# One attention-plus-SwiGLU kernel: a reordered opening and a later place for batch 1's key mixing

## The chip, the cores and the metric

The kernel runs on one core of a Trainium2 chip. The metric is the device time of one execution in microseconds (us). One execution was recorded by the profiler; its span, from the first to the last instruction, is shorter than its device time, because something lies around the span.

## The reference

There are four batches of 8 heads, 768 positions of 64 numbers each, and an 8 x 8 matrix `sort_net` per head. Five rounds of exp and of row and column normalisation turn `sort_net` into P. P mixes the eight blocks of 96 positions of K and of V; each block of Q then attends to the mixed block, and a SwiGLU feed-forward layer takes all heads side by side.

```
for _ in range(5):
    P = exp(P - max(P)); P = P / sum(P, axis=-1); P = P / sum(P, axis=-2)
k_sorted = einsum('bhij,bhjcd->bhicd', P, k_blocks)
v_sorted = einsum('bhij,bhjcd->bhicd', P, v_blocks)
attn = softmax(scale * q_block @ k_sorted_block.T)
x = (attn @ v_sorted_block)           # 3072 tokens x 512 (8 heads x 64)
out = (silu(x @ w_gate) * (x @ w_val)) @ w_out     # 512 -> 1536 -> 512
```

## The kernel before

**Stages.** The tokens fall into eight passes of 384, `ffn(0)` to `ffn(7)`: pass n is half n % 2 of batch n // 2. A pass needs `xts[(b, half)]`, the attention output with features on partitions. Attention runs in units, `(b, u)` for u from 0 to 7: four blocks of two heads. A unit goes through `qk` (scores, 8 matmuls, then an exp on ScalarE), `av` (8 matmuls, then a reciprocal and a multiplication on VectorE), and a transpose (4 matmuls and a copy) into `xts`. Units 0 to 3 of a batch feed its first pass, units 4 to 7 its second.

**Mixing.** Before a batch's units, K and Q are mixed and transposed together by `kq_chunk` (L230: two matmuls for each of n positions into one PSUM tile, then one copy `drain` on VectorE, "v", or ScalarE, "s"), and V by `v_chunk` (L240: one matmul for each of n features, then a drain in the same way). Batch 0 is mixed in the opening, lines 456 to 474. Batch 1 is mixed inside the second pass: `kqs(1, ...)` gives three pairs of key chunks, and `vs(v_chunk, 16, ...)` four chunks of values.

**What sets the order.** TensorE and GpSimd follow the program exactly (a manual schedule). In the opening VectorE and ScalarE do too; from line 525 on they are ordered by the framework's scheduler, which is not spelled out in the code. In the passes, `merge(main, side)` (L551) puts side work between the steps of a pass: each main step has a cost (0.65 for a gate or value group of four matmuls, 0.87 for a third of an output tile), the costs are added up, and a side step is put in as soon as the sum reaches its due time. These costs only set the order. In `ffn(1)` the outputs of pass 0 (`outp`, L384) come after the value group m = 3, 7 and 11, in three parts each.

**PSUM.** Tags "a" and "b" are two double-bank tiles, shared by the mixing chunks, scores and AV results; each new use waits until the last one is drained. "gen" is three banks, used in turn by gate, value and some output tiles. "x" is one bank, for transposes.

**Transfers.** GpSimd issues all loads, with a cast to bf16, in program order: V, Q and K of batch 0, the gate and value weights in 12 pieces, K, V and Q of batch 1 (`load_q(1, 0, C)`, L144), the output weights `wo_sb` in one piece (L145), and then K of batches 2 and 3 (`kp`, L95). The four copies `vch<-v` of batch 1 (L120) follow on GpSimd.

**Unread matmuls.** `fill(idle_ps, n)` (L415) issues n matmuls of 128 x 512 whose results nobody reads.

```
kq_chunk(1, ...) reads kq_tiles[1]: rows 0-63 from load_k(1), rows 64-127 from load_q(1)
outp(n, t3, part) reads h_tiles[n] and wo_sb
```

Of the kernel before, what the change touches and what calls it, by code (L numbers as in the profile page):

```python
# [17 lines left out]
def kernel(  # L18
# [158 lines left out]
    def pair_tile(name, tag):  # L177
        return psum.tile([128, 1024], FP32, name=name, tag=tag)

    def bank_tile(name, tag="gen"):  # L180
        return psum.tile([128, 512], FP32, name=name, tag=tag, bufs=3 if tag == "gen" else 1)
# [29 lines left out]
    def drain(eng, dst, src):  # L211
        if eng == "v":
            nc.vector.tensor_copy(dst, src)  # L213
        else:
            nc.scalar.copy(dst, src)  # L215
# [3 lines left out]
    def kqt_tile(b):  # L219
        if b not in kqts:  # L220
            kqts[b] = kqp.tile([128, 2 * H2 * NB * C + 32], BF16, name=f"kqt{b}", tag="kqt")
        return kqts[b]
# [3 lines left out]
    def chunk_tile(name, n, tag):  # L226
        return pair_tile(name, tag) if n == 2 else bank_tile(name, tag)

    def kq_chunk(b, at, n, eng, tag):
        dst = kqt_tile(b)[:, 0:2 * GI * C].rearrange("p (n c) -> p n c", c=C)  # L230
        rm = rmix[b].rearrange("p two a g i -> p two (a g i)")
        tp = chunk_tile("tkq", n // 8, tag).rearrange("p (l n) -> p l n", n=2 * GI)
        for lc in range(n):
            for two in range(2):
                nc.tensor.matmul(tp[two * D:(two + 1) * D, lc, :],  # L235
                                 lhsT=kq_tiles[b][:, at + lc, :],
                                 rhs=rm[:, two, :], start=True, stop=True)
        drain(eng, dst[:, :, at:at + n], tp.transpose([0, 2, 1]))
# [25 lines left out]
    def scores(b, u, tag):  # L264
        half, g = divmod(u, H2)
        k_sb, k_at, q_sb, q_at = ((kqts[b], 0, kqts[b], GI * C) if b < 2 else
                                  (kqts["p"], (b - 2) * GI * C, kqts["q"], (b - 2) * GI * C))
        if tag == "gen":
            wide = None
            pss = [bank_tile("qk"), bank_tile("qk")]  # L270
        else:
            wide = pair_tile("qk", tag).rearrange("p (two n) -> p two n", two=2)
            pss = [wide[:, 0], wide[:, 1]]
        for i4 in range(4):
            at = (g * NB + half * 4 + i4) * C
            for two in range(2):
                lo = two * D
                nc.tensor.matmul(pss[two][:, i4 * C:(i4 + 1) * C],  # L278
                                 lhsT=k_sb[lo:lo + D, k_at + at:k_at + at + 128],
                                 rhs=q_sb[lo:lo + D, q_at + at:q_at + at + C],  # L280
                                 start=True, stop=True)
        return wide, pss

    def exps(b, u, wide, pss):
        n = ecount[0] % 8
        ecount[0] += 2
        if wide is None:
            for two in range(2):
                nc.scalar.activation(e_all[:, n + two, 0:4 * C], pss[two][0:C, 0:4 * C], AF.Exp, scale=scale)
        else:  # L290
            nc.scalar.activation(e_all[:, n:n + 2, 0:4 * C], wide[0:C, :, 0:4 * C], AF.Exp, scale=scale)  # L291
        es[(b, u)] = [e_all[:, n, :], e_all[:, n + 1, :]]

    def qk(b, u, tag="b"):
        exps(b, u, *scores(b, u, tag))

    def av(b, u, tag="a"):
        half, g = divmod(u, H2)
        vt = vts[b // 2][:, b % 2].rearrange("p (h i) e -> p h i e", h=H)
        av_ps = pair_tile("av_ps", tag).rearrange("p (two n) -> p two n", two=2)  # L300
        o = av_ps[:, :, 0:4 * (D + 1)].rearrange("p two (i e) -> p two i e", e=D + 1)
        for two in range(2):
            e = es[(b, u)][two]
            for i4 in range(4):
                nc.tensor.matmul(o[:, two, i4, :], lhsT=e[:, i4 * C:i4 * C + 128],  # L305
                                 rhs=vt[:, 2 * g + two, half * 4 + i4, :],
                                 start=True, stop=True)
        r_sb = ssp.tile([C, 2, 4, 1], FP32, name="r_sb", tag="r")
        nc.vector.reciprocal(r_sb, o[0:C, :, :, D:D + 1])  # L309
        st = ssp.tile([C, 4, 2, D], BF16, name="st", tag="st")  # L310
        nc.vector.tensor_tensor(st.rearrange("p i two d -> p two i d"), o[0:C, :, :, 0:D],  # L311
                                r_sb.to_broadcast([C, 2, 4, D]), op=ALU.mult)
        sts[(b, u)] = st

    def xt_tile(tag, n):
        bank = psum.tile([128, 1024], BF16, name="x_ps", tag=tag, bufs=3 if tag == "gen" else 1)
        return bank[:, 0:n * 4 * C].rearrange("p (g a b) -> p g a b", g=n, b=C)

    def x_to(dst, b, u):
        st = sts.pop((b, u))  # L320
        for i4 in range(4):
            nc.tensor.transpose(dst[:, i4, :], st[:, i4].rearrange("p a b -> p (a b)"),
                                ident[0:C, 0:C])
# [89 lines left out]
    idle_ps = bank_tile("idle_ps", "x")  # L413

    def fill(tile, n):  # L415
        for _ in range(n):
            nc.tensor.matmul(tile, lhsT=warm_sb[:, 0:128], rhs=warm_sb, start=True, stop=True)  # L417
# [37 lines left out]
    fill(idle_ps, 2)  # L455
    v_chunk(0, 0, 8, "v", "gen")
    v_chunk(0, 8, 16, "s", "a")
    fill(idle_ps, 2)
    v_chunk(0, 24, 16, "v", "b")
    fill(idle_ps, 2)  # L460
    v_chunk(0, 40, 8, "s", "gen")
    v_chunk(0, 48, 8, "v", "gen")
    v_chunk(0, 56, 8, "s", "gen")
    kq_chunk(0, 0, 16, "v", "a")
    kq_chunk(0, 16, 16, "s", "b")
    fill(idle_ps, 1)
    kq_chunk(0, 32, 8, "s", "gen")
    kq_chunk(0, 40, 8, "s", "gen")
    kq_chunk(0, 48, 8, "v", "gen")
    fill(idle_ps, 1)  # L470
    kq_chunk(0, 56, 16, "v", "b")
    fill(idle_ps, 1)
    kq_chunk(0, 72, 16, "s", "a")
    kq_chunk(0, 88, 8, "v", "gen")
    for b in range(1, B):
        mix_of(b, w_sb)
# [4 lines left out]
    idle_ps = bank_tile("idle_ps")  # L481
# [3 lines left out]
    av(0, 1, "b")  # L485
    fill(idle_ps, 1)
    xts[(0, 0)] = xtp.tile([128, H2, TW], BF16, name="xt0_0", tag="xt")
    x01 = xt_tile("x", 2)
    x_to(x01[:, 0], 0, 0)
    fill(idle_ps, 1)  # L490
    qk(0, 3, "gen")
    av(0, 2, "a")
    x_to(x01[:, 1], 0, 1)
    drain("s", xts[(0, 0)][:, 0:2, :], x01.rearrange("p g a b -> p g (a b)"))
    fill(idle_ps, 2)
# [32 lines left out]
    def units(b, us, ats):  # L528
        us = list(us)
        todo = []  # L530
        for n, at in enumerate(ats):
            u, u2 = us[2 * n:2 * n + 2]
            held = []
            todo.append((at, lambda u=u, u2=u2, held=held: (qk(b, u, "b"), held.append(scores(b, u2, "a")))))
            todo.append((at + 1.3, lambda u2=u2, held=held: exps(b, u2, *held[0])))
            for w, tag, t in ((u, "b", 1.9), (u2, "a", 3.6)):
                if b < 2:
                    todo.append((at + t, lambda w=w, tag=tag: av(b, w, tag)))
                    todo.append((at + t + 3.1, lambda w=w: drain("v", *xtr(b, w))))
                else:  # L540
                    todo.append((at + t, lambda w=w, tag=tag: (av(b, w, tag), x_dma(b, w))))
        return todo

    def kqs(b, ats):
        return [(at, lambda n=n: (kq_chunk(b, n * 32, 16, "v", "b"), kq_chunk(b, n * 32 + 16, 16, "s", "a")))
                for n, at in enumerate(ats)]

    def vs(f, size, ats):
        return [(at, lambda m=m: f(1, m * size, size, "sv"[m % 2], "ba"[m % 2])) for m, at in enumerate(ats)]

    def merge(main, side):  # L551
        done, k = 0.0, 0
        side = sorted(side, key=lambda t: t[0])
        for c, f in main:
            f()
            done += c
            while k < len(side) and side[k][0] <= done:
                side[k][1]()
                k += 1
        while k < len(side):  # L560
            side[k][1]()
            k += 1

    def ffn(n):
        todo = []
        for m in range(NFC):
            if n > 0 or m > 1:
                todo.append((0.65, lambda m=m: gate(n, m)))
            if n > 0 or m > 0:
                todo.append((0.65, lambda m=m: value(n, m)))  # L570
            if n > 0 and m % 4 == 3:
                for part in range(3):
                    todo.append((0.87, lambda m=m, part=part: outp(n - 1, m // 4, part)))
        return todo
# [7 lines left out]
    q_cast(3)  # L582
    both = slice(0, 128)
    merge(ffn(0), units(0, range(4, 8), (0.0, 5.6)))
    merge(ffn(1), kqs(1, (0.3, 2.6, 4.9)) + vs(v_chunk, 16, (6.2, 7.3, 8.4, 9.5)) + units(1, range(4), (11.0, 15.6)))
    for s in range(4):
        copy_v(nc.gpsimd, 1, both, s)
    nc.vector.memset(kqt_tile("p")[:, 2 * GI * C:], 0.0)
# [42 lines left out]
```

The softmax here doesn't subtract the row's maximum and nothing guards it: scores larger than these inputs give would overflow.

## Time and profile before

| what | value |
|---|---|
| five executions | 254.05, 254.5, 254.67, 255.87, 256.28 us |
| their median | 254.67 us |
| the profiled execution | 254.5 us |
| its span | 252.4 us |
| TensorE busy | 240.7 us (95% of the span) |
| VectorE busy | 159.4 us (63%) |
| ScalarE busy | 110.5 us (44%) |
| GpSimd busy | 52.0 us (21%) |
| granted TensorE clock | 1.000 |

Stretches of the trace, in us from the span's start:

| stretch | what TensorE does | TensorE busy, us |
|---|---|---|
| 12.71 to 21.37 | batch 0's mixing with unread matmuls | 8.54 |
| 21.37 to 28.50 | first four units, first gate and value groups | 6.44 |
| 28.50 to 47.14 | pass 0 with units 4 to 7, then gate 0 of pass 1 | 18.50 |
| 47.14 to 49.19 | waits | 0.00 |
| 49.19 to 57.55 | batch 1's key mixing between the groups of pass 1 | 8.32 |
| 57.55 to 66.90 | outputs of pass 0, value mixing, first scores of batch 1 | 9.09 |
| 66.90 to 81.14 | the rest of pass 1 | 14.18 |
| 81.14 to 252.4 | passes 2 to 7 and the last outputs | 167.78 |

A line of the timeline gives start, duration, engine, source line, operation, output and inputs, the number of instructions and, in brackets, how long the engine was idle before it and what ended that. A matmul's end is modelled, so the duration of a group runs a little past the start of the next one; the time that a group takes is read from start to start.

### The profile page before, as it was taken

The page shows a single profiled execution, that of the slowest core. Times are in us where ns is not written, and L with a number is a line of the kernel's source. Part 1 is how long each engine was busy: PE and PEld are TensorE (multiplying, and loading weights), DVE is VectorE, ACT ScalarE, POOL GpSimd, SP SyncE. Part 2 cuts the span into 40 slices and gives each one's busy share as a digit, 9 for nine tenths or more (in the row PEclk, how much of TensorE's full clock was granted, in tenths as well). Part 3 has the DMA queues.
Part 4 walks back from the last instruction along what each step waited for, and adds up shares of the span by engine and source line. Part 5 has one row for each costly group of instructions (what it writes and reads, how often), then busy time and mean ns, then how long its engine had stood idle before and what let it go on. Part 6 is the DMA issues. An engine that isn't in the chain of part 4 may idle for free.

```text
span 252.4 us, 6061 instructions
## 1 busy us (share of the span) xinstructions
PE 240.7 (95%) x2574; PEld 143.3 (57%) x2574; DVE 159.4 (63%) x342; ACT 110.5 (44%) x187; POOL 52.0 (21%) x46
## 2 busy tenths in 40 slices
PE   5799999699999999999999999999999999999994
PEld 5275566466555666656656555555555565555543
DVE  6767788685757866758668458545854685456700
ACT  3966644255542543455544433443434243332311
POOL 7838430799069100000000000000000000000000
PEclk9999999999999999999999999999999999999999
DMA  5949999999999176110113112111111111100122
GB/s 101 212 78 161 196 216 219 194 222 216 230 156 153 42 168 130 42 44 3 42 21 85 42 41 57 51 44 32 60 57 42 34 57 57 44 7 34 44 83 84
DMA packets 37866, 23.98 MB, mean 95 GB/s; under 512 B 26064, under 2 KB 34000, under 8 KB 37328
## 3 DMA queue, kind: packets, MB, share of 16 engines
q0 software_dynamic: 21328, 14.16, 38.3%
q1 hardware_dynamic: 16512, 9.45, 13.0%
q8 instruction: 20, 0.33, 0.5%
q14 instruction: 6, 0.05, 0.1%
HBM read 28.32 MB, written 7.86 MB: 143 GB/s over the span
## 4 chain that ended last, share of the span: by engine, by line
PE 74%; DMA 15%; DVE 3%; POOL 3%; issue 2%; ACT 1%; DVEq 0%; POOLq 0%
PE o_ps L391 23%; PE v_ps L374 21%; PE g_ps L356 20%; DMA kq<-in_q_dram 7%; DMA kq<-in_k_dram 5%; DMA wg_sb<-in_moe_w_gate_dram 4%; PE tkq L235 3%; PE av_ps L305 2%; PE qk L278 2%; PE tv L257 1%; DVE gs_sb L366 1%; PE o_ps L407 1%; DVE vt L213 1%; POOL wg_sb L107 1%; POOL wv_sb L107 1%
## 5 line engine op out<-in xcount | busy, mean ns | idle before, releaser
L366 DVE SCALAR_TENSOR_TENSOR gs_sb<-th_sb,g_ps 128x384 bf16<-128x384 bf16 x96 | 52.8, 550 | 52.9 <-ACT th_sb L364 50.7
L374 PE MATMUL v_ps<-xt,wv_sb 128*128 128x384 bf16 x380 | 77.3, 326 | 0.3
L356 PE MATMUL g_ps<-xt,wg_sb 128*128 128x384 bf16 x376 | 76.5, 326 | 0.0
L364 ACT ACTIVATE th_sb<-g_ps 128x384 bf16<-128x384 f32 x96 | 47.2, 491 | 57.9 <-PE g_ps L356 54.9
L391 PE MATMUL o_ps<-wo_sb,h 128*128 128x512 bf16 x276 | 64.5, 379 | 0.0
L379 DVE SCALAR_TENSOR_TENSOR h<-v_ps,gs_sb 128x384 bf16<-128x384 f32 x96 | 53.3, 555 | 6.9 <-DVE gs_sb L366 0.5
L374 PEld LDWEIGHTS <-wv_sb 128*128 128x128 bf16 x380 | 35.4, 97 | 23.6 <-issue 1.5
L356 PEld LDWEIGHTS <-wg_sb 128*128 128x128 bf16 x376 | 34.6, 97 | 22.9
L391 PEld LDWEIGHTS <-h 128*128 128x128 bf16 x276 | 26.0, 98 | 27.7
L396 ACT COPY o_sb<-o_ps 128x512 f32<-128x512 f32 x23 | 13.5, 586 | 51.4 <-PE o_ps L391 51.4
L120 POOL COPY vch<-v 64x1536 bf16<-64x1536 bf16 (+1 forms) x10 | 28.1, 2850 | 18.4 <-DMA v<-in_v_dram 10.1
L291 ACT ACTIVATE e_all<-qk 96x768 bf16<-96x768 f32 x30 | 22.5, 802 | 6.2 <-PE qk L278 6.2
L311 DVE TENSOR_TENSOR st<-av_ps,r_sb 96x512 bf16<-96x512 f32 x32 | 21.7, 679 | 0.2
L305 PEld LDWEIGHTS <-e_all 96*128 96x128 bf16 x256 | 12.2, 98 | 5.1 <-ACT e_all L291 0.9
L305 PE MATMUL av_ps<-vt,e_all 96*128 96x65 bf16 x256 | 13.5, 194 | 0.2 <-ACT e_all L291 0.2
L213 DVE CAST vt<-tv 96x1024 bf16<-96x1024 f32 (+1 forms) x9 | 9.8, 1101 | 4.3 <-PE tv L247 4.3
L215 ACT CAST vt<-tv 96x1024 bf16<-96x1024 f32 (+1 forms) x9 | 9.1, 1030 | 5.6 <-PE tv L247 2.9
L309 DVE RECIPROCAL r_sb<-av_ps 96x8 f32<-96x8 f32 x32 | 6.4, 199 | 6.2 <-PE av_ps L305 6.1
L235 PE MATMUL tkq<-rmix,kq 128*64 128x64 bf16 x384 | 7.4, 197 | 2.0 <-DMA kq<-in_q_dram 2.0
L417 PE MATMUL idle_ps<-warm_sb 128*128 128x512 bf16 x30 | 9.2, 394 | 0.0
L215 ACT CAST kqt<-tkq 128x1024 bf16<-128x1024 f32 (+1 forms) x7 | 6.0, 894 | 7.0 <-PE tkq L235 7.0
L213 DVE CAST kqt<-tkq 128x1024 bf16<-128x1024 f32 (+1 forms) x7 | 7.5, 1069 | 2.6 <-PE tkq L235 2.4
(79 smaller groups left out, 135.6 us busy)
## 6 DMA issues: line engine op xcount, KB each, us to landing
out_dram<-o_sb SPq DMA_DIRECT2D x23, 256.0 KB, 2.0
v<-in_v_dram POOLq DMA_DIRECT2D x3, 768.0 KB, 14.3
kq<-in_q_dram POOLq DMA_DIRECT2D x2, 768.0 KB, 13.6
wg_sb<-in_moe_w_gate_dram POOLq DMA_DIRECT2D x6, 256.0 KB, 9.4
wv_sb<-in_moe_w_val_dram POOLq DMA_DIRECT2D x6, 256.0 KB, 10.0
wo_sb<-in_moe_w_out_dram POOLq DMA_DIRECT2D x1, 1536.0 KB, 23.6
kp<-in_k_dram POOLq DMA_DIRECT2D x2, 768.0 KB, 26.9
q_scr<-in_q_dram POOLq DMA_DIRECT2D x2, 768.0 KB, 21.1
```

What stands on the lines that cost most here:

```text
L120: eng.tensor_copy(dst, src.transpose([0, 2, 1]))
L213: nc.vector.tensor_copy(dst, src)
L215: nc.scalar.copy(dst, src)
L291: nc.scalar.activation(e_all[:, n:n + 2, 0:4 * C], wide[0:C, :, 0:4 * C], AF.Exp, scale=scale)
L305: nc.tensor.matmul(o[:, two, i4, :], lhsT=e[:, i4 * C:i4 * C + 128], rhs=vt[:, 2 * g + two, half * 4 + i4, :], start=True, stop=True)
L311: nc.vector.tensor_tensor(st.rearrange("p i two d -> p two i d"), o[0:C, :, :, 0:D], r_sb.to_broadcast([C, 2, 4, D]), op=ALU.mult)
L356: nc.tensor.matmul(g_ps, lhsT=wg_sb[:, kc, ts(m, 128)], rhs=xt[:, kc, :], start=(kc == 0), stop=(kc == NKC - 1))
L364: nc.scalar.activation(th_sb, g_ps, AF.Tanh, scale=0.5)
L366: nc.vector.scalar_tensor_tensor(gs_sb, th_sb, 1.0, g_ps, op0=ALU.add, op1=ALU.mult)
L374: nc.tensor.matmul(v_ps, lhsT=wv_sb[:, kc, ts(m, 128)], rhs=xt[:, kc, :], start=(kc == 0), stop=(kc == NKC - 1))
L379: nc.vector.scalar_tensor_tensor(h_tiles[n][:, m, :], v_ps, 0.5, gs_tiles.pop(m), op0=ALU.mult, op1=ALU.mult)
L391: nc.tensor.matmul(o_ps, lhsT=h_w[:, m, ts(t3, 128)], rhs=wo_sb[:, m, :], start=(m == 0), stop=(m == NFC - 1))
```

## The change

There are three edits, all of them to the order in which TensorE is given work; no matmul that is read is added or removed.

1. In the opening the two fills of two between the value chunks go (four matmuls), and one more unread matmul is put ahead of `kq_chunk(0, 32, ...)`, of `kq_chunk(0, 56, ...)` and of `kq_chunk(0, 88, ...)` (three matmuls).
2. The scores of unit 3 and the AV of unit 2 now come ahead of the transposes of unit 0; one unread matmul between them goes.
3. In `ffn(1)` the due times of batch 1's key mixing go from 0.3, 2.6, 4.9 to 2.4, 4.6, 6.8, those of its value mixing from 6.2, 7.3, 8.4, 9.5 to 7.8, 8.8, 9.8, 10.8, and those of its two unit pairs from 11.0 and 15.6 to 11.7 and 16.2.

```diff
     v_chunk(0, 0, 8, "v", "gen")
     v_chunk(0, 8, 16, "s", "a")
-    fill(idle_ps, 2)
     v_chunk(0, 24, 16, "v", "b")
-    fill(idle_ps, 2)
     v_chunk(0, 40, 8, "s", "gen")
     v_chunk(0, 48, 8, "v", "gen")
     v_chunk(0, 56, 8, "s", "gen")
     kq_chunk(0, 0, 16, "v", "a")
     kq_chunk(0, 16, 16, "s", "b")
-    fill(idle_ps, 1)
+    fill(idle_ps, 2)
     kq_chunk(0, 32, 8, "s", "gen")
     kq_chunk(0, 40, 8, "s", "gen")
     kq_chunk(0, 48, 8, "v", "gen")
-    fill(idle_ps, 1)
+    fill(idle_ps, 2)
     kq_chunk(0, 56, 16, "v", "b")
     fill(idle_ps, 1)
     kq_chunk(0, 72, 16, "s", "a")
+    fill(idle_ps, 1)
     kq_chunk(0, 88, 8, "v", "gen")
...
     xts[(0, 0)] = xtp.tile([128, H2, TW], BF16, name="xt0_0", tag="xt")
+    qk(0, 3, "gen")
+    av(0, 2, "a")
     x01 = xt_tile("x", 2)
     x_to(x01[:, 0], 0, 0)
-    fill(idle_ps, 1)
-    qk(0, 3, "gen")
-    av(0, 2, "a")
     x_to(x01[:, 1], 0, 1)
...
-    merge(ffn(1), kqs(1, (0.3, 2.6, 4.9)) + vs(v_chunk, 16, (6.2, 7.3, 8.4, 9.5)) + units(1, range(4), (11.0, 15.6)))
+    merge(ffn(1), kqs(1, (2.4, 4.6, 6.8)) + vs(v_chunk, 16, (7.8, 8.8, 9.8, 10.8)) + units(1, range(4), (11.7, 16.2)))
```

The order that `merge` makes of this in `ffn(1)` (g and v are gate and value groups, o a third of an output tile, kq a pair of key chunks, vs a value chunk, U a pair of units' scores):

```
before: g0 kq0 v0 g1 v1 kq1 g2 v2 g3 v3 kq2 o o vs0 o vs1 g4 vs2 v4 g5 vs3 v5 g6 U v6
after:  g0 v0 g1 v1 kq0 g2 v2 g3 v3 kq1 o o kq2 o vs0 g4 v4 vs1 g5 v5 vs2 g6 vs3 v6 U
```

## The prediction

> **What bounds the kernel now.** I read the busy shares first (TensorE 95%), then the chain of waits in order of time, then the transfers, then the timelines of the four engines around 47 us. Starts and durations below are us from the span's start. The chain shows which end comes last; its part from 28 to 62 us:
>
> ```profile
> 21.05 9.96 DMA wg_sb<-in_moe_w_gate_dram
> ...
> 31.30 17.76 DMA kq<-in_q_dram
> ...
> 49.19 1.20 PE tkq L235 x64
> ...
> 57.61 1.83 PE o_ps L391 x8
> ```
>
> Up to 49.19 the end is set by transfers. The opening is not on this path. Q of batch 1 is issued at 31.30 and lands at 31.30 + 17.76 = 49.06; the key mixing starts 0.13 later. TensorE's timeline shows the one large gap behind it, 2.05 us, and what follows:
>
> ```profile
> 46.33 0.81 PE L356 MATMUL g_ps<-xt,wg_sb 128*128 128x384 bf16 x4
> 49.19 1.20 PE L235 MATMUL tkq<-rmix,kq 128*64 128x64 bf16 x64 [2.05 <-DMA kq<-in_q_dram]
> ...
> 56.41 1.20 PE L235 MATMUL tkq<-rmix,kq 128*64 128x64 bf16 x64
> 57.55 1.90 PE L391 MATMUL o_ps<-wo_sb,h 128*128 128x512 bf16 x8
> ...
> 65.96 0.35 PE L278 MATMUL qk<-kqt 64*128 64x96 bf16 x8 [0.26 <-DVE vt L213]
> ```
>
> What matters next is the transfer behind Q. GpSimd's timeline has the issues, the page's list of transfers the times to landing:
>
> ```profile
> 31.30 0.52 POOL L98 DMA_DIRECT2D kq<-in_q_dram  x1 [0.77 <-DMA wg_sb<-in_moe_w_gate_dram]
> 32.82 1.05 POOL L145 DMA_DIRECT2D wo_sb<-in_moe_w_out_dram  x1 [1.00 <-DMA wv_sb<-in_moe_w_val_dram]
> ...
> 45.49 11.20 POOL L120 COPY vch<-v 64x1536 bf16<-64x1536 bf16 x4 [9.46 <-DMA v<-in_v_dram]
> ```
>
> ```profile
> wo_sb<-in_moe_w_out_dram POOLq DMA_DIRECT2D x1, 1536.0 KB, 23.6
> ```
>
> The output weights land at 32.82 + 23.6 = 56.42. The spacing is that of one queue served in order: V at 30.00 + 15.4 = 45.4 (its copy starts at 45.49), Q 768 KB later at 49.06 (3.66 us), the output weights 1536 KB later at 56.42 (7.36 us), about 213 GB/s each. Before, the first output group starts at 57.55, 1.1 us after they landed, so no wait shows.
>
> **What the Trainium skill says.** "DMA: Bandwidth & Descriptors", section "Why a DMA increments its semaphore by 16 and not by 1": only the full count means that all data landed. The trace agrees in so far as TensorE starts 0.13 after the landing of Q; so `wo_sb`, one transfer, can't be used in part. Same page, "SWDGE vs HWDGE vs iDMA": GpSimd's transfers have one queue; the spacing above agrees. "PSUM — Partial Sum Buffer", section "Engine vs sequencer instructions": VectorE's and ScalarE's queues are strictly first in, first out, so a drain waits behind whatever was queued ahead of it. "TensorE: Matmul & The Clock Gate", Part 1: about 3.4 us of idling halves TensorE's clock. This trace has gaps of up to 2.05 us and a granted clock of 1.000 in every stretch.
>
> **The change part by part.**
>
> *Opening, unread matmuls.* Two between start-to-start neighbours take 0.43 (14.61 to 15.14 with the changeover 0.53), so 0.216 each. Four go between the value chunks, three come in the key mixing, one goes at the transposes: 30 become 28, 0.43 us of TensorE less. But the value and key drains of VectorE follow each other almost without a gap from 14.71 (idle only 0.48 and 0.26 in six us), so what counts is that the value drains start about 0.43 earlier and the key drains about 0.6. Both ends: 0 (ScalarE's drains end last anyway) to 0.9 earlier. I take 0.6.
>
> *Opening, units 2 and 3 ahead of the transposes.* Unit 3's scores no longer stand behind four transposes (0.17) and one unread matmul (0.22): its exps can start up to 0.4 earlier, and TensorE's wait of 0.32 for the fourth unit's VectorE work at 27.34 shrinks. The transposes of unit 0 come about 0.55 later, but their copy needs unit 1's transposes too, which come after AV 2 in both orders. Ends: -0.3 (loss) to 0.6; I take 0.3 gained.
>
> Together TensorE reaches pass 1 some 0.9 earlier, with ends of -0.3 and 1.5. **None of this is worth anything:** the transfers don't wait for TensorE, so Q lands at 49.06 all the same. Nor do GpSimd's issues move, which wait for earlier landings; the wait put down to a gate matmul, 0.60 before `kp`, comes between two waits of the same size for weights.
>
> *Key mixing later.* Three groups (v0, g1, v1; 0.65 each, 1.95) now lie ahead of the wait. TensorE arrives at 47.14 + 1.95 = 49.09 without the opening's gain, at about 48.2 with it; the wait shrinks from 2.05 to 0.1, or to 1.0. Either way the mixing starts at 49.19 and 1.95 us of work are already done. That is the gain so far.
>
> *Where it goes.* In the new order only kq0, g2, v2, g3, v3, kq1 stand between Q and the first output groups. From the rows of before: 1.14 + 4 x 0.65 + 0.1 to 0.3 of changeover and bank wait + 1.14 = 5.0 to 5.2; TensorE reaches them at about 54.3. `wo_sb` lands at 56.42. So TensorE waits **2.2 us** and starts them at 56.55. Behind that wait stand all the rest of pass 1, kq2 included. Then two output groups 1.73, kq2 with its changeover 1.23, the third output group 0.87, vs0 0.47: 56.55 + 4.30 = 60.85. The kernel before has done exactly that set of work when vs1 starts, at 60.61. The gain of 1.95 is spent, and 0.24 more: kq2 used to fill the time before the weights landed.
>
> *The value mixing.* From here the same instructions remain, with two drains of 1.22 on VectorE. After: g4 60.85, v4 61.50, vs1 62.15, g5 62.62, v5 63.27, vs2 63.92, g6 64.39, vs3 65.04, v6 65.51, scores of unit 0 at 66.26. ScalarE is behind: kq2's drain 59.6 to 60.6, the output copy to 61.2, vs0's drain to 62.2, so the first tanh ends at 62.6. VectorE follows: gs4 to 63.17, h4 to 63.7, vs1's drain to 64.8, gs5 to 65.3, h5 to 65.8, gs6 (its tanh waits for vs2's drain, 66.1) to 66.65, vs3's drain to 67.85. The second score tile shares tag "a" with vs3 and can't start before 67.9; it wants to at 66.54. That wait is 1.35, in place of the 0.26 before, where vs3 had one group more between it and the scores. v6 and both scores are done at 68.16, against 66.90: from 60.85 that is 7.31 where before, from 60.61, it was 6.29, so 1.02 more and **1.26 us** in all. The rows of before support the method: the same sum gives 65.95 for vs3's drain, the trace 65.91.
>
> *Due times of the units.* The pairs move by two groups or one. AV 1 now has g8 (0.65) instead of an output third (0.87) before unit 3's scores want its tile: its reciprocal and multiplication end 1.13 after it (70.44 to 71.57), the scores want it after about 1.03: 0.1. The last transposes now stand right before pass 2's first gate group, whose last matmul wants the copy 0.49 later; the copy takes 0.2 + 0.35: 0.1. Against this the small waits of before at 74.3 and 77 go or move (0.23). Bounds: -0.3 to 0.7; I take 0. The moved steps issue no transfer but the output stores on SP's queue, which come later by as much and are waited for by nobody here. Passes 2 to 7 have TensorE busy nearly throughout; nothing gives the loss back.
>
> **Sum** against the profiled execution, 254.5 (span 252.4 and 2.1 around it): 254.5 - 1.95 (groups ahead of Q) + 2.19 (output weights and the order behind them) + 1.02 (value mixing and the second score tile) + 0 (units) = 255.76. The median of the runs shown, 254.67, is 0.17 higher, well inside their scatter of 2.2, so I stay with **255.8**.
>
> **The rivals.**
> - *VectorE takes vs3's drain ahead of gs6.* VectorE's order is the scheduler's here; at 68.74 of before a reciprocal runs ahead of an h that comes earlier in the program, so it does fill gaps. Then vs3 is drained at 65.8 to 67.05, the second score tile starts at 67.1 and the loss is 0.45: 255.0. Against it: in the one near tie of before (64.22) the gate step went ahead of the drain.
> - *The gain survives.* If the output weights were there by 54.3, all that follows came 2.25 earlier, with the same wait at the scores: 1.26 lost becomes 0.99 gained, 253.7. Against it: three landings that fit one rate.
> - *Slower.* The end of pass 1 becomes a chain through VectorE: AV 3 after g11, its multiplication behind h11, the transposes after the last output third, the copy, and then pass 2's first gate. It decides once VectorE is over 0.5 late there; at one gate and one value step late (1.1) it costs 0.6 beyond the sum, with two score tiles waiting likewise 1.0: 256.6.
> - *The clock.* With fewer unread matmuls between the value chunks TensorE may idle enough to be throttled. It costs nothing until TensorE is over 2.3 late at pass 1 (0.1 and the 2.2 of the second wait); I give it almost nothing, as no gap of 3.4 us arises.
>
> **How the numbers follow.** Likeliest course 0.50 (255.4 to 256.3), drain taken early 0.23 (254.7 to 255.3), gain survives 0.10 (253.2 to 253.9), slower chain 0.15 (256.3 to 257), clock 0.02. What a measurement here can tell from no change is about 0.5%, 1.27 us: 253.4 to 255.94. The likeliest course lies three fifths within (0.30) and two fifths slower (0.20); the early drain (0.23) and half of the surviving gain (0.05) are within; the slower chain and the clock are slower (0.17). So faster 0.05, same 0.58, slower 0.37. A range of 254.2 to 256.7 leaves out the surviving gain and part of the slower chain.
>
> **What would show it.** After: a wait of 0 to 1.3 for `kq<-in_q_dram` that ends at about 49.2; a new wait of about 2 for `wo_sb<-in_moe_w_out_dram` that ends near 56.5; the unit scores at L278 waiting 0.5 to 1.4 for `vt`; first gate groups (L507) up to a us earlier. The prediction is wrong if the output weights land before 55, if Q's landing moves with TensorE, or if the new waits are made up for later.

## The result and the profile after

| | kernel before | changed kernel |
|---|---|---|
| runs | 80 | 43 |
| median | 254.08 us | 254.99 us |
| lowest, highest | 253.11, 257.18 us | 254.01, 258.1 us |
| profiled execution | 254.5 us (span 252.4) | 256.76 us (span 254.7) |
| mean granted clock of the profiled execution | 1.000 | 0.993 |

The changed kernel takes 1.0036 times as long as the kernel before, with a 95% interval of 1.0021 to 1.0052: about 0.9 us more. Ratios, here and below, leave out the runs more than 1.5% above the fastest of the same kernel and are not quotients of the medians shown. Its profiled execution lies 1.8 us above its median. Why can be seen below: a loss that only half of its runs have falls into it.

The chain of waits of the changed kernel no longer runs through Q but through the output weights (start, duration, what):

```profile
21.80 10.11 DMA wv_sb<-in_moe_w_val_dram
31.91 0.28 issue
32.20 24.39 DMA wo_sb<-in_moe_w_out_dram
56.59 0.05 issue
56.63 2.74 PE o_ps L391 x8
```

TensorE's timeline of the changed kernel between 45 and 70 us:

```profile
45.73 0.81 PE L356 MATMUL g_ps<-xt,wg_sb 128*128 128x384 bf16 x4
...
47.72 0.81 PE L374 MATMUL v_ps<-xt,wv_sb 128*128 128x384 bf16 x4
49.13 1.20 PE L235 MATMUL tkq<-rmix,kq 128*64 128x64 bf16 x64 [0.60 <-DMA kq<-in_q_dram]
...
53.16 1.20 PE L235 MATMUL tkq<-rmix,kq 128*64 128x64 bf16 x64
56.63 2.74 PE L391 MATMUL o_ps<-wo_sb,h 128*128 128x512 bf16 x8 [2.27 <-DMA wo_sb<-in_moe_w_out_dram]
59.30 1.86 PE L235 MATMUL tkq<-rmix,kq 128*64 128x64 bf16 x64
61.09 1.04 PE L391 MATMUL o_ps<-wo_sb,h 128*128 128x512 bf16 x4
...
62.44 0.81 PE L356 MATMUL g_ps<-xt,wg_sb 128*128 128x384 bf16 x4
...
68.78 0.35 PE L278 MATMUL qk<-kqt 64*128 64x96 bf16 x8 [0.60 <-DVE vt L213]
69.05 0.82 PE L356 MATMUL g_ps<-xt,wg_sb 128*128 128x384 bf16 x4
```

Rows of the kernel before that the text compares with it:

```profile
50.33 0.82 PE L374 MATMUL v_ps<-xt,wv_sb 128*128 128x384 bf16 x4
...
52.38 1.20 PE L235 MATMUL tkq<-rmix,kq 128*64 128x64 bf16 x64
53.52 0.82 PE L356 MATMUL g_ps<-xt,wg_sb 128*128 128x384 bf16 x4
...
59.28 0.63 PE L247 MATMUL tv<-vmix,vch 128*128 128x64 bf16 x16
...
66.90 0.81 PE L356 MATMUL g_ps<-xt,wg_sb 128*128 128x384 bf16 x4
```

The wait for Q has gone from 2.05 to 0.60, and its end has stayed: the key mixing starts at 49.13, before at 49.19. A wait of 2.27 for the output weights has come, which ends at 56.63. Behind it two things are longer than their rows of before. Eight output matmuls take 2.67 from start to start (56.63 to 59.30) where they took 1.73 (57.55 to 59.28), or 1.82 ahead of a key pair (e1 below), and the key pair takes 1.79 (59.30 to 61.09) where it took 1.14 (52.38 to 53.52). The stretches of one us tell why; the columns are length, busy time of TensorE's matmuls, of its weight loads, of VectorE, ScalarE and GpSimd, the granted clock, the transfers' share and GB/s:

```profile
56.60:57.60 1.00, 0.97 (x5) 0.50 (x6) 0.00 (x0) 0.00 (x0) 0.88 (x2) 0.97 0.93 197
57.60:58.60 1.00, 1.00 (x4) 0.31 (x3) 0.00 (x0) 0.00 (x0) 1.00 (x2) 0.50 0.94 197
58.60:59.60 1.00, 1.00 (x14) 0.30 (x14) 0.00 (x0) 0.00 (x0) 1.00 (x1) 0.50 0.99 209
59.60:60.60 1.00, 1.00 (x46) 1.00 (x42) 0.19 (x1) 0.00 (x0) 1.00 (x2) 0.50 0.98 209
60.60:61.60 1.00, 1.00 (x27) 0.72 (x24) 1.00 (x1) 0.39 (x1) 1.00 (x1) 0.82 0.99 209
```

The granted clock falls to a half about 0.9 us after the matmuls resume, and comes back 3.4 us later (from about 57.54 to 60.96). That costs 0.85 at the output matmuls and 0.65 at the key pair, 1.50 in all.

The difference of the two profiled executions is then complete. Value group v6 and the first two units' scores are done at 69.05, before at 66.90: 2.15 later. From there to the first gate group of pass 2 both take the same, 14.24 (69.05 to 83.29, and 66.90 to 81.14). The spans differ by 2.3.

Over all recorded executions the clock is a dividing line. A fall of 3.4 us to one half makes the mean granted clock of a run about 0.993. Of the 44 executions of the changed kernel whose clock was recorded 22 lie below 0.9965, with a median of 256.26; the other 22 have 254.62. In the comparisons below, the kernel before has 46 such runs in 173, so it pays a price of the clock as well, in a quarter of its runs; its other 127 have a median of 254.12. With the clock held, the changed kernel is thus about 0.5 longer (the runs are not all from one chip). A run's mean clock does not tell where in the run the clock fell; only a profile does.

### The profile page after: what moved, and what is told of

It is laid out like the page before. It is cut to its first block, busy times and chain, and to the rows that moved or that the text cites. A ratio compares the mean times of both kernels' runs of the same rounds, so it can differ in the third digit from the quotient of the medians.

```text
span 254.7 us, 6059 instructions
## 1 busy us (share of the span) xinstructions
PE 241.5 (95%) x2572; PEld 143.9 (56%) x2572; DVE 159.7 (63%) x342; ACT 110.5 (43%) x187; POOL 51.9 (20%) x46
## 4 chain that ended last, share of the span: by engine, by line
PE 71%; DMA 18%; DVE 4%; POOL 3%; ACT 1%; issue 1%; DVEq 0%; POOLq 0%
PE o_ps L391 23%; PE v_ps L374 20%; PE g_ps L356 19%; DMA wo_sb<-in_moe_w_out_dram 10%; DMA kq<-in_k_dram 4%; DMA wv_sb<-in_moe_w_val_dram 4%; PE av_ps L305 2%; PE tkq L235 2%; PE qk L278 2%; PE tv L257 1%; POOL wg_sb L107 1%; PE o_ps L407 1%; DVE vt L213 1%; POOL wv_sb L107 1%; DVE h L379 1%
## 5 line engine op out<-in xcount | busy, mean ns | idle before, releaser
L391 PE MATMUL o_ps<-wo_sb,h 128*128 128x512 bf16 x276 | 65.4, 383 | 2.3 <-DMA wo_sb<-in_moe_w_out_dram 2.3
L235 PEld LDWEIGHTS <-kq 128*64 128x64 bf16 x384 | 7.5, 119 | 3.5 <-issue 3.4
L235 PE MATMUL tkq<-rmix,kq 128*64 128x64 bf16 x384 | 8.4, 204 | 0.6 <-DMA kq<-in_q_dram 0.6
```

The costliest lines, as they stand in the source:

```text
L235: nc.tensor.matmul(tp[two * D:(two + 1) * D, lc, :], lhsT=kq_tiles[b][:, at + lc, :], rhs=rm[:, two, :], start=True, stop=True)
L391: nc.tensor.matmul(o_ps, lhsT=h_w[:, m, ts(t3, 128)], rhs=wo_sb[:, m, :], start=(m == 0), stop=(m == NFC - 1))
```

## The experiments

Each was timed against the kernel before on the same chip. "Clock fell" counts the executions with a mean granted clock under 0.9965.

| experiment | median | before | ratio, 95% interval | clock fell |
|---|---|---|---|---|
| e1: unread matmuls in the wait for the output weights | 254.81 | 254.59 | 0.9999, 0.9978 to 1.0019 | 1 of 22 |
| e2: later due times only | 254.73 | 254.59 | 1.0022, 0.9995 to 1.0049 | 5 of 22 |
| e3: opening only | 254.54 | 254.59 | 0.9993, 0.9969 to 1.0018 | 11 of 22 |
| e4: change, output weights in three pieces | 252.75 | 254.59 | 0.9919, 0.9890 to 0.9948 | 0 of 10 |
| e5: kernel before, unread matmuls in the wait for Q | 254.43 | 254.20 | 0.9995, 0.9975 to 1.0015 | 1 of 22 |
| e6: kernel before, output weights in three pieces | 254.35 | 254.20 | 0.9999, 0.9976 to 1.0023 | 4 of 22 |
| e7: third key pair ahead of the outputs | 253.85 | 254.20 | 0.9977, 0.9953 to 1.0000 | 1 of 22 |
| e8: e4 with both unit pairs one step later | 253.13 | 254.20 | 0.9943, 0.9921 to 0.9965 | 3 of 22 |
| e9: e4 again | 253.00 | 254.29 | 0.9940, 0.9916 to 0.9963 | 2 of 13 |
| e10: e4 with the old opening | 253.13 | 254.29 | 0.9938, 0.9918 to 0.9957 | 0 of 21 |
| e11: e4 with the unit pairs one and two steps later | 252.32 | 254.29 | 0.9905, 0.9871 to 0.9939 | 0 of 8 |

The theory, of which each recorded text below calls its own form theory A: the change moves TensorE's wait from Q to the output weights, so its gain is spent; the idle stretch there lets the clock fall; VectorE's drain of the fourth value chunk adds a smaller wait. The rivals: VectorE alone is the cause; the opening carries a part; the weights don't matter.

### Is the price of the clock real?

**e1** fills the new wait.

```diff
-        o_ps = o_tiles[n]
+        o_ps = o_tiles[n]; fill(o_ps, 8 if (n, t3, part) == (0, 0, 0) else 0)
```

> The changed kernel with eight unread 128x512 matmuls put into the 2.27 us wait for the output weights (8 x 0.216 = 1.73 us, so they end before the weights land); the orders of all other engines are the same. Theory A (half of the loss is the clock, which falls to 0.50 for 3.4 us after the idle stretch, in about half of the runs): granted clock 1.000 in every run, the output groups after the wait at 0.216 a matmul, time about 254.6, that is 0.4 to 0.7 above the kernel before. Theory B (the loss is only the wait and VectorE's drains, the clock is a side effect without price): no change against the changed kernel, about 255.0, with some runs still near 256.

Its timeline (a few matmul records are missing from the traces, so x7 stands for eight):

```profile
53.47 1.20 PE L235 MATMUL tkq<-rmix,kq 128*64 128x64 bf16 x64
54.61 1.90 PE L417 MATMUL o_ps<-warm_sb 128*128 128x512 bf16 x7
57.24 1.89 PE L391 MATMUL o_ps<-wo_sb,h 128*128 128x512 bf16 x8 [0.73 <-DMA wo_sb<-in_moe_w_out_dram]
59.06 1.20 PE L235 MATMUL tkq<-rmix,kq 128*64 128x64 bf16 x64
```

The unread matmuls end before the weights land and hold up nothing; the output matmuls behind them take 1.82 again, and the clock falls in 1 of 22 runs instead of in half. The time over all runs is that of the kernel before (0.9999). Theory A had it 0.4 to 0.7 above, but the kernel before pays for the clock in a third of its runs here (21 of 63). Among runs with a held clock alone the medians are 254.75 and 254.29, so about 0.5 of loss is still there, near the 0.56 worked out below. Theory B, a clock without a price, speaks for a ratio near 1.0036, which lies outside e1's interval; the changed kernel itself was not timed again on this chip.

**e5** does the same for the kernel before, in its wait for Q.

```diff
-        tp = chunk_tile("tkq", n // 8, tag).rearrange(...)
+        raw = chunk_tile("tkq", n // 8, tag); fill(raw[:, 0:512], 8 if (b, at) == (1, 0) else 0); tp = raw.rearrange(...)
```

> The kernel before with eight unread 128x512 matmuls (1.73 us) put into its wait for Q of batch 1; the orders of all other engines are the same. Theory A (an idle stretch of 2 to 3.5 us in pass 1 makes the clock fall for 3.4 us, at a price of 1.6 to 1.9, in a third of this kernel's runs): runs with a clock of 0.993 fall from a third to a tenth or none, median and mean about 254.2, 0.3 to 0.6 below the mean of the kernel before. Theory B (runs with a fallen clock are longer because their transfers land late): the long runs stay as many, mean within 0.2.

The clock falls in 1 of 22 runs instead of 18 of 75, and the longest run goes from 257.85 to 255.42. The mean, though, falls only from 254.64 to 254.49, and the median does not fall at all. 17 of the 75 runs of the kernel before are longer than the longest of e5, so the long runs do not stay, as theory B had it, and they go with the clock; but theory A's 0.3 to 0.6 on the mean did not come. Among runs with a held clock e5 even has the longer median, 254.40 against 254.06. Whether the unread matmuls cost something, or whether runs with a late Q are now among those with a held clock, stays open; in its profile they are done 0.61 before the mixing starts.

### Which part does what?

**e2** has only the due times, **e3** only the opening (the two diffs of the change, one at a time).

> Only the later due times, with the opening of the kernel before. Theory A (the opening's gain is swallowed by the wait for Q): as the changed kernel, 254.6 to 255.2; the wait for Q 0.1 instead of 0.6, the wait for the output weights 2.2 as before; clock falls in perhaps fewer runs, since TensorE idles 0.5 less. Rival (the opening carries a part of the loss): 254.0 to 254.3.

> Only the two edits of the opening, with the due times of the kernel before. Theory A: TensorE reaches pass 1 about 0.65 earlier and waits for Q 2.7 instead of 2.05; nothing is gained, and the clock falls more often, so 254.1 to 255.0. Rival (the opening's gain reaches the end): 253.4 to 253.6.

e2 has a wait for the output weights too, but a smaller one in its profiled execution, 0.57 and not the 2.2 expected: TensorE reaches the key mixing only at 49.64, after Q, and the weights land early, at 55.40.

```profile
55.45 1.90 PE L391 MATMUL o_ps<-wo_sb,h 128*128 128x512 bf16 x7 [0.57 <-DMA wo_sb<-in_moe_w_out_dram]
```

Its ratio of 1.0022 can't be told from that of the change or from none. e3 brings nothing that can be seen, 0.9993, with an interval of about 0.6 us to either side. The earlier arrival lengthens the wait for Q; whether the clock falls more often for it can't be told from 11 of 22 beside 21 of 63. Its profiled execution shows a long wait, to which a Q that landed 0.85 later than in the kernel before adds, and the clock behind it:

```profile
50.04 1.20 PE L235 MATMUL tkq<-rmix,kq 128*64 128x64 bf16 x64 [3.48 <-DMA kq<-in_q_dram]
51.17 1.29 PE L374 MATMUL v_ps<-xt,wv_sb 128*128 128x384 bf16 x4
52.26 1.49 PE L356 MATMUL g_ps<-xt,wg_sb 128*128 128x384 bf16 x4
53.54 1.44 PE L374 MATMUL v_ps<-xt,wv_sb 128*128 128x384 bf16 x4
54.91 1.20 PE L235 MATMUL tkq<-rmix,kq 128*64 128x64 bf16 x64
```

Three groups of four matmuls take 3.74 (51.17 to 54.91) where they took 2.05 before (50.33 to 52.38): 1.7 for one fall.

### Did the output weights eat the gain?

**e4** loads them in three pieces, one for each third of an output tile, at the same place of the queue. **e6** is the control: the same edit on the kernel before.

```diff
-    nc.gpsimd.dma_start(out=wo_sb, in_=wo_dram)
+    for m in (0, 4, 8): nc.gpsimd.dma_start(out=wo_sb[:, m:m + 4], in_=wo_dram[:, m:m + 4])
```

> The changed kernel with the output weights loaded in three pieces of 512 KB, one for each third of an output tile, in the same place of the queue; the orders of the other engines are the same. Theory A (the wait for the whole of the output weights ate the gain): first piece lands about 2.45 us after Q, at 51.5, before it is wanted at 54.3; no wait or a few tenths, no fall of the clock there, and 1.0 to 1.8 less than the kernel before: 252.4 to 253.1. Rival (pass 1 is bound by VectorE's drains whatever the weights do): 254.0 to 254.6.

> Control: the kernel before with the output weights in three pieces, the only change. Theory A (the weights aren't waited for in the kernel before): no change, within 0.3. Rival (pieces are better in themselves, because the queue then serves Q earlier, which would explain the gain of the changed kernel with three pieces): 0.5 or more below the kernel before, with Q landing before 48.5.

e4's timeline, where Q landed at 48.09 and the mixing waited for nothing:

```profile
48.56 1.20 PE L235 MATMUL tkq<-rmix,kq 128*64 128x64 bf16 x64
...
52.59 1.20 PE L235 MATMUL tkq<-rmix,kq 128*64 128x64 bf16 x64
53.72 1.90 PE L391 MATMUL o_ps<-wo_sb,h 128*128 128x512 bf16 x7
55.55 1.20 PE L235 MATMUL tkq<-rmix,kq 128*64 128x64 bf16 x64
...
64.41 0.35 PE L278 MATMUL qk<-kqt 64*128 64x96 bf16 x8 [0.60 <-DVE vt L213]
```

There is no wait at all ahead of the output groups, which now follow the second key pair without a pause, and the kernel is 0.8% shorter than the kernel before. The same edit does nothing for the kernel before (0.9999), which never waited for these weights. The clock is not the whole of it: runs with a held clock alone have 252.76, against 254.29 of the kernel before. So the gain of the later due times is real, and the single transfer of the output weights took it. **e9** is e4 once more.

> The changed kernel with the output weights in three pieces once more, for a comparison on the same chip with the two others. Theory A: 0.6 to 1.0% below the kernel before, as the first time.

0.9940; the two intervals overlap.

**e7** leaves the transfer whole and puts work into the wait instead: `kqs(1, (2.4, 3.7, 5.1))`, so that the third key pair stands ahead of the outputs.

> The changed kernel with the key mixing due at 2.4, 3.7 and 5.1 in place of 2.4, 4.6 and 6.8, so that the third pair comes ahead of the first output group and lies in the wait for the output weights; the weights are one transfer. Theory A: the wait shrinks from 2.27 to about 1.1, the rest comes 1.1 earlier, the clock falls in few runs: 253.3 to 253.8. Rival (VectorE's drains bind pass 1): 254.3 to 254.8.

At 253.85 it ends just above what theory A gave, with an interval that just reaches 1. In its profiled execution no wait for the weights is listed, but the third pair stops for 0.81 in its midst, for nothing that the profile shows, and the outputs start at 55.65:

```profile
54.99 0.73 PE L235 MATMUL tkq<-rmix,kq 128*64 128x64 bf16 x35 [0.81 <-issue]
```

The stop ends 0.10 after the weights land (30.99 + 23.9 = 54.89), as closely behind a landing as the listed waits for transfers end (0.04 to 0.17). So it may be the same wait in another place; this, and whether it comes in every run, stays open.

### Does the opening count once nothing waits for the weights?

**e10** is e4 with the opening of the kernel before.

> The later due times and the output weights in three pieces, with the opening of the kernel before. Theory A (the opening's 0.65 us only shorten or lengthen the wait for Q): TensorE reaches the key mixing at about 49.1, as Q lands, so within 0.3 of the kernel with the new opening. Rival (without the wait for the output weights the opening's gain reaches the end): 0.4 to 0.7 longer than it.

0.9938, beside 0.9940 of e9 on the same chip: no gain of 0.4 to 0.7 is seen, though the intervals of 0.2% to either side leave room for some tenths. The profiles are not as theory A had them: TensorE reaches the key mixing at 49.61, 0.68 after Q landed (30.53 + 18.4 = 48.93), so that in this execution an earlier opening could have counted, while e9 waits 0.37 for a later Q.

### The wait for VectorE

**e8** and **e11** start from e4 and move the units of batch 1: due at 12.3 and 16.8, and at 12.3 and 17.5, in place of 11.7 and 16.2.

> The changed kernel with the output weights in three pieces and the units of batch 1 due at 12.3 and 16.8 in place of 11.7 and 16.2, so that a gate group lies between the sixth value group and the first scores. Theory A (the second score tile waits 0.6 for VectorE's drain of the fourth value chunk): that wait goes, 0.4 to 0.6 less than with three pieces alone, about 252.3. Rival (the later units make the end of pass 1 wait for the last transposes): 252.7 to 253.3.

> The changed kernel with three pieces and the units of batch 1 due at 12.3 and 17.5: the first pair one group later than in the change, the second two, so that a gate and a value group and one more gate group lie between the second AV and the third and fourth scores. Theory A: neither of the two waits of 0.6 for VectorE (for the fourth value drain, for the second AV's result) is left, 0.4 to 0.6 below three pieces alone. Rival (the last transposes then come too late for pass 2): no gain or 0.5 longer.

In e8 the wait for the fourth value drain is gone and another of the same size has come, now for the second unit's AV result at the third and fourth unit's scores:

```profile
72.18 0.34 PE L278 MATMUL qk<-kqt 64*128 64x96 bf16 x8 [0.58 <-DVE st L311]
```

The time doesn't fall: 0.9943 lies beside 0.9940 of e9, and 253.13 in the range that the rival gave, though the wait that came is not the rival's. e11 gives that unit more room too, and no wait for VectorE is listed between 45 and 90 us. It takes 252.32 us, 0.7 less than e9, and is the shortest of all: 0.9905 of the kernel before, with an interval of 0.9871 to 0.9939. It beats both kernels.

## Why the prediction came out as it did

- *Opening worth nothing*: right. It was put at 0.9 earlier at pass 1, and is 0.60 (gate 0 of pass 1 starts at 45.73, before at 46.33). None of it is seen at the end (e3, e10), within about half a us. "Nor do GpSimd's issues move" does not hold for this profile: Q was issued 0.44 earlier (30.86). But its issues lie between 29.64 and 31.30 over all profiles, and Q landed within 0.1 of before.
- *1.95 gained at Q, spent at the output weights*: right to the tenth. Predicted 49.19 and 56.55, measured 49.13 and 56.63; a wait of 2.2 predicted, 2.27 measured. That it fits to the tenth is in part luck, since Q's landing lies anywhere in 1.9 us over the profiles (below). e4 and e6 together show that this wait is the cause.
- *The value mixing, 1.02*: the step failed in size. "gs6 (its tanh waits for vs2's drain, 66.1) to 66.65, vs3's drain to 67.85" put the gate's step ahead of the drain. In the changed kernel the scheduler has the drain first, as in the first rival:

```profile
67.03 0.56 DVE L379 SCALAR_TENSOR_TENSOR h<-v_ps,gs_sb 128x384 bf16<-128x384 f32 x1
67.51 1.21 DVE L213 CAST vt<-tv 96x1024 bf16<-96x1024 f32 x1
68.64 0.54 DVE L366 SCALAR_TENSOR_TENSOR gs_sb<-th_sb,g_ps 128x384 bf16<-128x384 bf16 x1
```

  The second score tile waits 0.60 and not 1.35, and the stretch from g4 to g7 takes 6.61 (62.44 to 69.05; in e1, where the clock holds, 61.53 to 68.14, the same) instead of 7.31. The term is 0.32 instead of 1.02.
- *The clock, "almost nothing, as no gap of 3.4 us arises"*: this step failed. In the profile a fall followed a gap of 2.27, with one of 0.60 that ended five us ahead of it; half of the runs had a fall, and with the gap filled 1 of 22 (e1). It was also looked for only in the value mixing of the opening, where e8's profile does have a fall, and not at the new wait that the prediction itself had found. The Trainium skill's page "TensorE: Matmul & The Clock Gate", Part 1, names about 3.4 us of idling; the length of the fall (3.4) agrees with its window, the length of the gap that brings it about does not.
- *The sum*: 0.24 + 1.02 predicted. Measured in the profiled execution: 0.24 + 0.08 (the weights landed a little later) + 1.51 (clock, 0.01 of it at the third output group) + 0.32 (value mixing) = 2.15. Where the clock holds, 0.24 + 0.32 = 0.56 is left, near the 0.45 of the first rival, whose order of VectorE is the one that came; the medians of the runs with a held clock (254.62 and 254.12) agree. The 0.9 between the medians above is a mixture: half of the changed kernel's runs pay about 1.6 for the clock (256.26 and 254.62), and about a quarter of the runs before pay likewise.
- *The surviving gain*, 0.99 below: with the pieces it was 1.5 to 2.1 by the ratios of e9 and e4, and 1.1 to 1.5 where runs with a held clock are compared. (Its 253.7 counts from the median 254.67, the sum from 254.5.) Its term for the value mixing carried the same error of 0.7, and the kernel before pays for the clock in some of its runs.

So the time lay where it was forecast, near no change, and the main mechanism was right; but 0.7 too much on VectorE stood in for a price of the clock that was set at nothing. That these two errors nearly cancel is luck.

## What to carry to other kernels

When a wait for a transfer is filled with later work, look at what is next in the same queue: the work behind comes earlier by as much, and the next landing can take the whole gain. Cut that transfer into the pieces in which it is used, or keep independent work ahead of its first use. A wait that only moves can still cost more than before, when it brings TensorE's clock down. Unread matmuls that ended before the landing kept the clock up here in all but 1 of 22 runs, twice; that they are free on the average is not shown (e5).

## What the runs showed of the hardware

- The granted clock fell to 0.50 for 3.4 us (57.54 to 60.96 in the changed kernel, 51.4 to 54.8 in e3), and the fall began 0.9 and 1.3 us after the idle stretch had ended, in the midst of work. Gaps of 2.27 and 3.48 were followed by it, one of 2.05 was not; over all runs it came in 22 of 44, 46 of 173 and, with the waits filled, in 1 of 22 twice.
- The length of a gap alone did not decide. In e9 the clock fell in the opening, from about 9.9 to 13.3, just after a gap of 1.86 had ended at 9.73. The changed kernel's profile has the same gap at the same place (1.86, ended at 9.75), and its clock held there.
- The fall need not come in pass 1: in e8, too, it lies in the opening, from about 14.7 to 18.1, and TensorE then reached the key mixing of pass 1 at 49.82, after Q had landed, without a wait.
- The landings of one queue move from run to run by more than the effects studied here: Q landed between 48.0 and 49.9 in the profiled executions, the output weights, where they are one transfer, 6.8 to 8.3 later.
